# A routed expert layer behind attention on one core: the two largest experts in blocks of 384, 256 and a last one by count

## The chip, the cores and the metric

One core of a Trainium2 chip. The time is device microseconds (us) from the start of an execution to its end; lower is better. Engines are named as the profile names them: PE (TensorE, matrix products), DVE (VectorE), ACT (ScalarE), POOL (GpSimd) and SP (SyncE, which issues most transfers here).

## The reference, cut to what matters

```python
scores = np.matmul(z, z.transpose(0, 2, 1)) / S          # 8 batches, S = 1856, d_qk = 64
attn = np.maximum(scores, 0.0) ** 2
x = (u * np.matmul(attn, v)).reshape(8 * 1856, 256)       # 14848 tokens

g_logits = x @ w_group                                    # 4 groups, arg max, softmax weight g_w
e_logits = xg @ w_expert[g]                               # 4 experts in a group, arg max, weight e_w
h = np.maximum(xg[mask_e] @ w1[g, e], 0.0)                # 256 -> 1024
out[tok_idx] = (g_w * e_w)[:, None] * (h @ w2[g, e])      # 1024 -> 256
```

Every token goes to one of 16 experts. Routing the reference's inputs sends 1050 tokens to each of the two largest experts, 924 and 907 of them from the first seven batches, and from 1020 down to 749 to the others.

## The kernel before, in words

**Attention.** A batch is worked in four chunks of query columns (512, 512, 320, 512), a chunk in 15 key steps. In a step PE makes scores (`sc`), ACT and DVE square them and split them into a rounded part `ah` and a rest `al` (every product is made of float32 numbers split in two), and PE adds to the chunk's output `o`. `chunk_end` multiplies by `u` and sets the chunk's routing going. PE makes the logits (`pl`), ACT copies them to `lgp`, SP transposes them to `lgx`, DVE takes them up as `lgf` and works through some 15 small operations in `route`, PE counts places by three small products `pk`, DVE adds the experts' running ends `base` (`rk`, `df`, `di`), and POOL scatters the token rows, four indirect transfers a chunk, into a table `bucket` in device memory, in which each expert has a range of its own.

`defer(step, f)` and `gens` set at which key step each piece of this stands in the program; what falls behind the last step is put between the steps of the first expert blocks by `early`. The last chunk's logits stand 5 steps behind its end and its routing 8.

**Sorting ahead.** After the seventh batch `sort_experts` ranks the experts by their rows so far. For the two that lead, `base` is raised to at least 512 (`FRZ`), so that no token of the last batch can fall into their first 512 rows: these are settled, and can be read while the last batch is still routed.

**Experts.** `PARTS` cuts each expert, in that order of size, into blocks of rows. The last block of each of the first 15 experts has its width set at run time by the count: a `Switch` with 15 arms, one program text for each width in `WIDE` (512, 496, ... 288), the arms one behind the other. Blocks run in this order: the first of expert 0, the first of expert 1, then what is left of expert 0, of expert 1, and then expert after expert. A block is eight steps `f`. In a step PE makes six `ph` products (up, lines 775 to 777), ACT turns them into `hh` and DVE into the rest `hl`, and three steps later (`AHEAD`) PE makes six `y` products (down, lines 790 to 792). PE thus runs up to three steps ahead of ACT and DVE. At a block's end ACT copies `y` to `yp`, SP transposes to `yr`, DVE weights the rows (`yf`) and POOL scatters them to the output.

A block's input is loaded by `load_rows`: SP transposes rows of `bucket` into `xp` and loads `meta` (weight and token number). `join_block` makes of it, in three neighbouring steps of the block before, `meta` and `xf` (DVE), `xh_m` (ACT) and `xl_m` (DVE). The first step is f = 3, and f = 4 for the block in place `NEARLY` = 2. `more_rows` loads blocks ahead once no routing is left.

**The edge between the two halves.** In the second block, at f = 3, what is left of the routing is drained. Then DVE makes the counts (`counts`, `arms`, `overflow_count`), from which every engine reads the arm to take (`arm_i`) early in the third block. A region with arms holds its eight steps and the first three of the block behind it, and ends with a jump behind the last arm. PE alone is told of the arm beforehand (`hint`).

## Time and profile before

| | |
|---|---|
| median of 3 runs | 1501.58 us (1500.08 to 1502.61) |
| profiled execution | 1500.23 us, span of its instructions 1498.4 us |
| PE | busy 1479.4 us, 99% of the span, 7575 products |
| DVE, ACT, POOL | 74%, 67%, 20% of the span |
| attention | until about 829 us |
| experts 0 and 1 | about 817 to 928 us |
| granted PE clock | 1.00 of full from 0 to 1480 us |

Busy time of PE is an upper bound: ends of products are modelled, and consecutive products overlap. What a product costs is read from one start to the next. A bracket behind a row is the idle time ahead of it and what ended that.

### The profile page before, as it was taken

What the parts mean: (1) busy time and instruction counts of PE and PEld (TensorE: products, weight loads), DVE (VectorE), ACT (ScalarE), POOL (GpSimd) and SP (SyncE); (2) the same over time, 40 slices, a digit from 0 to 9 for tenths busy, and PEclk for the clock granted to TensorE, in tenths of its full rate; (3) what the DMA queues carried; (4) which work ended last, traced back from release to release, by engine and by line L of the source; (5) the groups of instructions that cost most, each with busy time, mean ns of one, the idle gap of its engine ahead of it and who ended that gap; (6) DMA issues with size and microseconds to landing.
All of it is one profiled execution on the core that took longest, in us unless ns stands there. A gap on an engine that the chain in (4) does not pass through costs nothing.

```text
span 1498.4 us, 23731 instructions
## 1 busy us (share of the span) xinstructions
PE 1479.4 (99%) x7575; PEld 1288.6 (86%) x7575; DVE 1109.1 (74%) x2659; ACT 1003.1 (67%) x1919; POOL 297.8 (20%) x346
## 2 busy tenths in 40 slices
PE   9999999999999999999999999999999999999997
PEld 7888888888888888888888789999888899889996
DVE  7888887888888988788898756666565666666663
ACT  7988888888888888888888435454444444444442
POOL 0011221121201111212103122222222222222222
PEclk9999999999999999999999999999999999999999
DMA  4423423333424334233584475776545765657541
GB/s 135 109 68 90 118 76 98 92 74 99 105 65 106 79 98 106 64 86 86 146 245 112 94 153 90 167 148 132 119 85 119 141 139 137 137 137 135 132 96 51
DMA packets 302314, 167.54 MB, mean 112 GB/s; under 512 B 238187, under 2 KB 281197, under 8 KB 301936
## 3 DMA queue, kind: packets, MB, share of 16 engines
q1 hardware_dynamic: 289616, 132.37, 40.5%
q0 software_dynamic: 11968, 30.91, 6.9%
q14 instruction: 283, 2.32, 0.6%
q8 instruction: 95, 1.56, 0.5%
q10 hardware_dynamic: 352, 0.39, 0.1%
HBM read 72.25 MB, written 41.60 MB: 76 GB/s over the span
## 4 chain that ended last, share of the span: by engine, by line
PE 88%; issue 3%; DVE 3%; ACT 2%; DMA 2%; SPq 1%; POOL 0%; DVEq 0%; POOLq 0%; ACTq 0%
PE o L388 13%; PE o L387 13%; PE o L390 12%; PE sc L348 6%; PE ph L777 6%; PE ph L775 6%; PE ph L776 6%; PE y L792 6%; PE y L790 6%; PE y L791 6%; PE sc L351 6%; DMA out_dram<-yf,meta 1%; PE pl L444 1%; PE pl L445 1%; DVE hl L780 0%
## 5 line engine op out<-in xcount | busy, mean ns | idle before, releaser
L779 ACT ACTIVATE hh<-ph 128x512 fp32r<-128x512 f32 (+11 forms) x296 | 149.4, 512 | 322.0 <-PE ph L777 241.1
L388 PE MATMUL o<-ah,vh 128*128 128x512 f32 (+1 forms) x960 | 354.5, 371 | 0.0
L387 PE MATMUL o<-ah,vl 128*128 128x512 f32 (+1 forms) x960 | 353.0, 370 | 0.9 <-DVE ah L364 0.7
L780 DVE SCALAR_TENSOR_TENSOR hl<-ph,hh 128x512 fp32r<-128x512 f32 (+11 forms) x296 | 169.2, 579 | 224.0 <-ACT hh L779 201.5
L367 DVE TENSOR_TENSOR al<-r,ah 128x512 fp32r<-128x512 f32 (+1 forms) x448 | 283.7, 634 | 14.8 <-ACT r L361 8.1
L352 ACT ACTIVATE r<-sc 128x512 f32<-128x512 f32 (+1 forms) x448 | 239.2, 553 | 79.9 <-PE sc L351 53.0
L390 PE MATMUL o<-al,vh 128*128 128x512 f32 (+1 forms) x896 | 274.5, 373 | 0.4 <-DVE al L367 0.3
L363 ACT ACTIVATE r<-r 128x512 f32<-128x512 f32 (+3 forms) x416 | 237.6, 590 | 4.2
L582 POOL DMA_INDIRECT bucket<-rows,di x120 | 128.3, 1069 | 546.4 <-DVE al L367 229.4
L795 POOL DMA_INDIRECT out_dram<-yf,meta x129 | 144.4, 1119 | 459.3 <-DVE yf L839 413.3
L777 PE MATMUL ph<-xl_m,w1h_e 128*128 128x512 f32 (+11 forms) x592 | 205.1, 346 | 1.7 <-DVE xl_m L756 1.7
L387 PEld LDWEIGHTS o<-ah,vl 128*128 128x128 f32 x960 | 180.3, 188 | 29.9 <-DVE ah L364 1.3
L775 PE MATMUL ph<-xh_m,w1l_e 128*128 128x512 f32 (+11 forms) x592 | 204.9, 346 | 1.0 <-issue 1.0
L388 PEld LDWEIGHTS o<-ah,vh 128*128 128x128 f32 x960 | 180.5, 188 | 28.4
L776 PE MATMUL ph<-xh_m,w1h_e 128*128 128x512 f32 (+11 forms) x592 | 204.6, 346 | 0.0
L792 PE MATMUL y<-hl,w_e 128*128 128x512 f32 (+11 forms) x576 | 199.8, 347 | 1.3 <-DVE hl L780 1.3
L790 PE MATMUL y<-hh,w_e 128*128 128x512 f32 (+11 forms) x576 | 199.4, 346 | 0.8 <-ACT yp L820 0.8
L791 PE MATMUL y<-hh,w_e 128*128 128x512 f32 (+11 forms) x576 | 199.3, 346 | 0.0
L364 DVE CAST ah<-r 128x512 fp32r<-128x512 f32 (+3 forms) x416 | 163.8, 399 | 41.9 <-ACT r L363 21.6
L390 PEld LDWEIGHTS o<-al,vh 128*128 128x128 f32 x896 | 162.8, 188 | 26.3 <-DVE al L367 1.3
L348 PE MATMUL sc<-zm,z2h 128*128 128x512 f32 (+1 forms) x480 | 178.5, 376 | 0.9 <-DVE r L356 0.4
L351 PE MATMUL sc<-zm,z2l 128*128 128x512 f32 (+1 forms) x448 | 166.5, 373 | 0.2 <-DVE z2l L902 0.2
(150 smaller groups left out, 2107.8 us busy)
## 6 DMA issues: line engine op xcount, KB each, us to landing
raw_e<-in_w_dram SPq DMA_DIRECT2D x64, 512.0 KB
ut<-in_uT_dram SPq DMA_DIRECT2D x24, 512.0 KB
vr<-in_v_dram SPq DMA_DIRECT2D x23, 512.0 KB
bucket<-padrow SPq DMA_DIRECT2D x16, 528.0 KB
zr<-in_zT_dram SPq DMA_DIRECT2D x47, 128.0 KB
ut<-in_uT_dram SPq DMA_DIRECT2D x8, 320.0 KB
vr<-in_v_dram SPq DMA_DIRECT2D x9, 256.0 KB
out_dram<-yf,meta POOLq DMA_INDIRECT x129
```

The source lines that it names most:

```text
L348: nc.tensor.matmul(ps[:, 0:w], z2h[:, ks], zm, start=True, stop=k == NKF)
L351: nc.tensor.matmul(ps[:, 0:w], z2l[:, ks], zm, start=False, stop=True)
L367: nc.vector.tensor_sub(out=al, in0=a, in1=f32(ah))
L387: nc.tensor.matmul(o, vl[:, dsl], ah, start=(at_ == 0), stop=False)
L388: newest[:] = [nc.tensor.matmul(o, vh[:, dsl], ah, start=False, stop=(at_ == NK - 1 and al is None))]
L390: nc.tensor.matmul(o, vh[:, dsl], al, start=False, stop=(at_ == NK - 1))
L775: nc.tensor.matmul(o, wt["l"][d][:, fs], xh[:, d, 0:W], start=(d == 0), stop=False)
L776: nc.tensor.matmul(o, wt["h"][d][:, fs], xh[:, d, 0:W], start=False, stop=False)
L777: nc.tensor.matmul(o, wt["h"][d][:, fs], xl[:, d, 0:W], start=False, stop=(d == ND - 1))
L790: nc.tensor.matmul(o, w2t[:, 1, dsl], hh[:, 0:W], start=(f == 0), stop=False)
L791: nc.tensor.matmul(o, w2t[:, 0, dsl], hh[:, 0:W], start=False, stop=False)
L792: nc.tensor.matmul(o, w2t[:, 0, dsl], hl_[:, 0:W], start=False, stop=(f == NF - 1))
```

## The change

`PARTS` gives experts 0 and 1 the blocks (384, 256, up to 512) of experts 2 to 4. With 1050 rows their last block has 410 rows and takes the arm of 416 (the seventh of 15); before, it had 282 and took 288, the fifteenth and last. The columns of the two experts stay the same: 512 + 256 + 288 = 384 + 256 + 416. `FRZ` settles 640 rows of expert 0 and 384 of expert 1, so three blocks can be loaded while routing goes on (`NFREE`). The last chunk's logits stand 7 steps behind its end instead of 5, its routing 10 instead of 8, and the drain and the counts at f = 6 of the second block. The later first step of a join, f = 4, falls to the fourth block, the last of expert 0.

```diff
-PARTS = ((512, 256, 512),) * 2 + ((384, 256, 512),) * 3 + ((512, 512),) * 8 + ((384, 512),) * 2 + ((512, 352),)
+PARTS = ((384, 256, 512),) * 5 + ((512, 512),) * 8 + ((384, 512),) * 2 + ((512, 352),)
...
-    FRZ = 512
-    assert all(p[0] == FRZ and len(p) > 1 for p in PARTS[:NEARLY])
+    NFREE = 3
+    FRZ = (640, 384)
+    assert sum(PARTS[0][:2]) == FRZ[0] and PARTS[1][0] == FRZ[1] and min(len(p) for p in PARTS[:NEARLY]) > 2
...
-        defer(s + (5 if last else 2), logits)
+        defer(s + (7 if last else 2), logits)
...
-        wait = 8 if last else 6
+        wait = 10 if last else 6
...
-        nc.vector.tensor_scalar(out=fz, in0=rank, scalar1=float(NEARLY), scalar2=float(FRZ),
+        nc.vector.tensor_scalar(out=fz, in0=rank, scalar1=1.0, scalar2=float(FRZ[0] - FRZ[1]),
                                 op0=ALU.is_lt, op1=ALU.mult)
         nc.vector.tensor_add(out=fz, in0=fz, in1=ebase)
+        fz1 = cst("sfz1", [P, NE])
+        nc.vector.tensor_scalar(out=fz1, in0=rank, scalar1=float(NEARLY), scalar2=float(FRZ[1]),
+                                op0=ALU.is_lt, op1=ALU.mult)
+        nc.vector.tensor_add(out=fz, in0=fz, in1=fz1)
         nc.vector.tensor_tensor(out=base, in0=base, in1=fz, op=ALU.max)
...
     def more_rows():
-        if not (deferred or gens):
-            while late["loaded"] < min(NB, late["joined"] + 2):
-                load_rows(late["loaded"])
-                late["loaded"] += 1
+        while late["loaded"] < min(NB if not (deferred or gens) else NFREE, late["joined"] + 2):
+            load_rows(late["loaded"])
+            late["loaded"] += 1
...
-            f0 = 4 if i + 1 == NEARLY else 3
+            f0 = 4 if i + 1 == NFREE else 3
...
-            if i + 1 == NEARLY and f == 3:
+            if i + 1 == NEARLY and f == 6:
...
-            if i + 1 < NB and f == (4 if i + 1 == NEARLY else 3) + 2:
+            if i + 1 < NB and f == (4 if i + 1 == NFREE else 3) + 2:
```

SP's queue behind the last chunk. `rows_3` and `lgx_3` are the last chunk's token rows and logits, `yr` the first block's output, `xp` and `meta` of 256 rows the input of the third block. Before:

```order
L434 DMA_TRANSPOSE rows_3_11160<-pl_3_11162 128x4x128 x4
L452 DMA_TRANSPOSE lgx_3_11164<-lgp_3_11163 128x8x48
L829 DMA_TRANSPOSE yr_0_11417<-yp_0_11414 128x4x128 x2
L829 DMA_TRANSPOSE yr_2_11423<-yp_2_11420 128x4x128 x2
L734 ISA
L734 DMA_TRANSPOSE xp_11445<-bucket 128x4x256
```

Now:

```order
L435 DMA_TRANSPOSE rows_3_11161<-pl_3_11163 128x4x128 x4
L453 DMA_TRANSPOSE lgx_3_11165<-lgp_3_11164 128x8x48
L739 ISA
L739 DMA_TRANSPOSE xp_11299<-bucket 128x4x256
L742 ISA
L742 DMA meta_11301<-bucket 128x2x2
L834 DMA_TRANSPOSE yr_0_11406<-yp_0_11403 128x4x128 x2
```

The third block's load moved ahead of the first block's output.

DVE in the second block. `hl_3` to `hl_7` are its steps; `meta`, `xf` and `xl_m` are the join of the third block; `cnt` is the first row of the counts, `ki` the last. Before:

```order
L1117 CAST ki<-tiles 128x1
L780 SCALAR_TENSOR_TENSOR hl_4_11485<-ph_4_11477,hh_4_11484 128x512
L763 TENSOR_TENSOR meta_11447<-meta_11447,none 128x2
L748 COPY xf_11495<-xp_11445 128x2x2x256
L780 SCALAR_TENSOR_TENSOR hl_5_11507<-ph_5_11499,hh_5_11506 128x512
L780 SCALAR_TENSOR_TENSOR hl_6_11525<-ph_6_11517,hh_6_11524 128x512
L756 TENSOR_TENSOR xl_m_11498<-xf_11495,xh_m_11497 128x2x256
```

Now:

```order
L785 SCALAR_TENSOR_TENSOR hl_3_11438<-ph_3_11430,hh_3_11437 128x384
L768 TENSOR_TENSOR meta_11301<-meta_11301,none 128x2
L753 COPY xf_11450<-xp_11299 128x2x2x256
L785 SCALAR_TENSOR_TENSOR hl_4_11462<-ph_4_11454,hh_4_11461 128x384
L785 SCALAR_TENSOR_TENSOR hl_5_11480<-ph_5_11472,hh_5_11479 128x384
L761 TENSOR_TENSOR xl_m_11453<-xf_11450,xh_m_11452 128x2x256
L785 SCALAR_TENSOR_TENSOR hl_6_11498<-ph_6_11490,hh_6_11497 128x384
L612 TENSOR_TENSOR cnt<-base,ebase 128x16
```

The counts moved behind the join and three steps back, the join a step ahead.

PE around the third chunk's places. `pk_2` are these, `ph_4` the first block's fifth step, `pl_3` the last chunk's logits. Before:

```order
L563 MATMUL pk_2_11112<-pre_2_11089,ones 128x16
L791 MATMUL y_0_11214<-hh_1_11187,w_e_0_9648 128x512
L792 MATMUL y_0_11214<-hl_1_11188,w_e_0_9648 128x512
L790 MATMUL y_1_11215<-hh_1_11187,w_e_0_9648 128x512
L791 MATMUL y_1_11215<-hh_1_11187,w_e_0_9648 128x512
L792 MATMUL y_1_11215<-hl_1_11188,w_e_0_9648 128x512
L444 MATMUL pl_3_11250<-xh_3_11152,whl 128x512
```

Now:

```order
L564 MATMUL pk_2_11113<-pre_2_11090,ones 128x16
L782 MATMUL ph_4_11233<-xl_m_10935,w1h_e_1_9644 128x384
L795 MATMUL y_0_11215<-hh_1_11188,w_e_0_9646 128x384
L796 MATMUL y_0_11215<-hh_1_11188,w_e_0_9646 128x384
L797 MATMUL y_0_11215<-hl_1_11189,w_e_0_9646 128x384
L795 MATMUL y_1_11216<-hh_1_11188,w_e_0_9646 128x384
```

Before, five products stood between the third chunk's last place count and `pl_3`; now the rest of that step and two whole steps do. The last chunk's own `pk_3` stands four steps behind `pl_3` now, and five before.

## Prediction

> **What bounds the kernel.** I read the page's busy times and its chain first.

> ```profile
> span 1498.4 us, 23731 instructions
> PE 1479.4 (99%) x7575; PEld 1288.6 (86%) x7575; DVE 1109.1 (74%) x2659; ACT 1003.1 (67%) x1919; POOL 297.8 (20%) x346
> PE 88%; issue 3%; DVE 3%; ACT 2%; DMA 2%; SPq 1%; POOL 0%; DVEq 0%; POOLq 0%; ACTq 0%
> ```

> PE sets the time: what the change gives or takes is products that cost more or less, and idle time of PE added or removed. The waits of PE, longest first, say how little idle time there is, and the timeline of PE where it is.

> ```profile
> PE ph L777 <- DVE xl_m L756: 1.7, 3, 1.2
> PE y L792 <- DVE hl L780: 1.3, 1, 1.3
> PE ph L775 <- issue: 1.0, 2, 0.6
> PE y L790 <- ACT yp L820: 0.8, 1, 0.8
> ```

> ```profile
> 765.70 0.50 PE L387 MATMUL o<-ah,vl 128*128 128x512 f32 x1 [0.31 <-DVE ah L364]
> ...
> 836.12 0.48 PE L444 MATMUL pl<-xh,whl 128*128 128x512 f32 x1 [0.68 <-DVE df L575]
> ...
> 848.56 0.18 PE L562 MATMUL pk<-pre,ones 128*128 128x48 bf16 x1 [0.33 <-DVE pre L544]
> ...
> 868.70 0.39 PE L777 MATMUL ph<-xl_m,w1h_e 128*128 128x256 f32 x1 [0.36 <-DVE xl_m L756]
> ...
> 871.23 0.37 PE L775 MATMUL ph<-xh_m,w1l_e 128*128 128x256 f32 x1 [0.40 <-issue]
> ...
> 888.15 0.29 PE L791 MATMUL y<-hh,w_e 128*128 128x288 f32 x1
> 889.71 0.40 PE L792 MATMUL y<-hl,w_e 128*128 128x288 f32 x1 [1.27 <-DVE hl L780]
> ...
> 902.33 0.37 PE L775 MATMUL ph<-xh_m,w1l_e 128*128 128x256 f32 x1 [0.58 <-issue]
> ...
> 924.02 0.44 PE L777 MATMUL ph<-xl_m,w1h_e 128*128 128x384 f32 x1 [1.16 <-DVE xl_m L756]
> ```

> So all the idle time that the two experts hold is seven short waits between 836 and 924 us. A wait costs more than its bracket: from 888.15 to 889.71 are 1.56 us where 0.13 are usual, 1.43 lost for a bracket of 1.27. I add 0.2 to each bracket: 0.9, 0.5, 0.6, 0.6, 1.5, 0.8 and 1.4, together 6.3 us. That is all the change can win here, 0.42%.

> **Products.** Each pair of rows below stands 24 products apart (512 and 384 wide) or 36 (288 and 416).

> ```profile
> 851.62 0.39 PE L775 MATMUL ph<-xh_m,w1l_e 128*128 128x512 f32 x1
> ...
> 857.06 0.39 PE L775 MATMUL ph<-xh_m,w1l_e 128*128 128x512 f32 x1
> ...
> 931.56 0.33 PE L775 MATMUL ph<-xh_m,w1l_e 128*128 128x384 f32 x1
> ...
> 935.72 0.33 PE L775 MATMUL ph<-xh_m,w1l_e 128*128 128x384 f32 x1
> ...
> 916.03 0.29 PE L775 MATMUL ph<-xh_m,w1l_e 128*128 128x288 f32 x1
> ...
> 920.77 0.29 PE L775 MATMUL ph<-xh_m,w1l_e 128*128 128x288 f32 x1
> ...
> 1213.80 0.35 PE L775 MATMUL ph<-xh_m,w1l_e 128*128 128x416 f32 x1
> ...
> 1220.52 0.35 PE L775 MATMUL ph<-xh_m,w1l_e 128*128 128x416 f32 x1
> ```

> That is 0.2267, 0.1733, 0.1317 and 0.1867 us a product; steps of twelve take 2.72, 2.08, 1.58 and 2.24. Before, 0.2267 + 0.1317 = 0.3583; now 0.1733 + 0.1867 = 0.3600. Times 96 products a block and two experts: **+0.3 us** (0 to +0.4, as the starts are rounded to 0.01). PE's work does not change; only the waits are left.

> ```profile
> 839.08 1.20 SPq L452 DMA_TRANSPOSE lgx<-lgp  x1
> 845.38 0.34 DVE L458 COPY lgf<-lgx 128x320 uint16<-128x320 uint16 x1
> 848.72 0.17 DVE L554 TENSOR_TENSOR rows<-ew,sm 128x4 f32<-128x4 f32 x1
> 857.24 0.17 DVE L611 TENSOR_TENSOR cnt<-base,ebase 128x16 f32<-128x16 f32 x1
> 860.06 0.17 DVE L633 CAST arm_i<-arm 128x15 int32<-128x15 f32 x1
> 865.34 0.16 DVE L763 TENSOR_TENSOR meta<-meta,none 128x2 int32<-128x2 int32 x1 [3.41 <-DMA meta<-bucket]
> 878.01 1.35 DVE L748 COPY xf<-xp 128x2048 uint16<-128x2048 uint16 x1
> 879.39 1.05 ACT L754 CAST xh_m<-xf 128x1024 fp32r<-128x1024 f32 x1 [1.08 <-DVE xf L748]
> 881.10 1.22 DVE L756 TENSOR_TENSOR xl_m<-xf,xh_m 128x1024 fp32r<-128x1024 f32 x1
> ```

> **The last logits (wait of 0.9 us).** `pl` needs the one bank that the third chunk's `pk` used, and DVE read it late. Two steps and a half, some 5 us, now stand between them in place of five products: **-0.9** (-0.9 to -0.5, if DVE lags).

> **The last places (0.5 us).** On DVE the chain from `lgf` to the row weights lasts 3.3 us (845.38 to 848.72) and starts behind a step's `hl`; `pk` stands behind two and a half more groups of six on PE. With six products at 1.04 instead of 1.36 that cover shrinks by three times 0.32, about 1.0; `hl` itself comes 0.2 sooner. **+0.8** (0 to +2; the upper end, if `lgx`, issued at 839.08 behind transposes that keep their place, is late for a routing that begins at about the same time as before: nine shorter steps for seven longer).

> **The third block's join (0.6 us).** DVE waited 3.41 us for a load that stood behind the drain and the first block's output on SP. It stands ahead of both now, four shorter steps before its use, and its rows wait for the third chunk's scatter alone: **-0.6** (-0.6 to 0).

> **Counts and arms (0.6 us at 871).** From `cnt` to `arm_i` are 3.0 us (857.24 to 860.06 and 0.17). They stand behind the seventh step of the second block in place of the fourth; PE reads the arm some one and a half steps later, about 4 us, so a little under 1 us is left of some 10. The read itself stays: **0** (0 to +1).

> **The fourth block's join.** Its first step is f = 4 instead of 3, in a block whose steps take 1.44 us. `xf`, `xh_m` and `xl_m` take 1.35 + 1.05 + 1.22 = 3.6 and one `hl` between; before, they ended at 882.32 for a region that starts about 882.7. From the step's own `hl`, some 1.5 us into it, they now end about 6.2 us into what are 6.1 to the first use: **+0.3** (0 to +1). Its load waits for the last scatter, but has four steps more than the one before.

> ```profile
> 889.20 0.46 DVE L780 SCALAR_TENSOR_TENSOR hl<-ph,hh 128x288 fp32r<-128x288 f32 x1 [6.17 <-ACT yp L820]
> ...
> 914.89 1.19 DVE L780 SCALAR_TENSOR_TENSOR hl<-ph,hh 128x288 fp32r<-128x288 f32 x3 [3.82 <-ACT hh L779]
> ...
> 1003.63 0.54 DVE L780 SCALAR_TENSOR_TENSOR hl<-ph,hh 128x368 fp32r<-128x368 f32 x1 [5.75 <-ACT hh L779]
> ```

> **Into the arm (1.5 us at 889).** These are DVE's first rows in the arms of experts 0, 1 and 3: it is away 3.8 to 6.2 us while PE lives on its three steps' lead. Three ups and three downs of the narrow block are 3 x (0.79 + 0.71) = 4.5 us of cover; at 416 wide 3 x (1.12 + 0.71) = 5.5, and one more up of 1.12 in place of 0.79: 1.3 us more. Against it, DVE leaves up to 1 us later, behind the later join. Expert 3's arm, away 5.75, put PE to no wait of 0.3 us, and the waits have only one of this kind. **-1.1** (-1.5 to 0).

> **Out of the arm.**

> ```profile
> 903.75 0.42 DVE L780 SCALAR_TENSOR_TENSOR hl<-ph,hh 128x256 fp32r<-128x256 f32 x1 [1.92 <-ACT hh L779]
> ...
> 978.29 0.56 DVE L780 SCALAR_TENSOR_TENSOR hl<-ph,hh 128x384 fp32r<-128x384 f32 x1 [3.39 <-ACT hh L779]
> ...
> 1069.25 0.69 DVE L780 SCALAR_TENSOR_TENSOR hl<-ph,hh 128x512 fp32r<-128x512 f32 x1 [4.43 <-ACT hh L779]
> ```

> Behind expert 0's arm, the last of the fifteen, DVE is back after 1.92 us; behind those of experts 2 and 4, with other arms' text between them and the exit, after 3.39 and 4.43. Experts 0 and 1 now leave from the seventh arm, so 1.5 to 2.5 us more. Behind expert 1 follow steps of 2.08, as behind expert 2, where PE did not wait. Behind expert 0 follow five of 1.44: about 4.3 us of lead against DVE's return, then `xf` of 1.35 and a weight split ahead of the next `xl_m`. **+0.6** (0 to +2.5); the 0.8 at 902.33 stays. [...]

> **Expert 2's first join (1.4 us at 924).** Its three steps now lie in a region with steps of 2.24 instead of 1.58, 2 us more: **-1.4** (-1.4 to -0.5).

> **Sorting.** Two more DVE operations while attention runs, where PE lost 0.5 at 765.70; each like this row:

> ```profile
> 761.41 0.17 DVE L671 TENSOR_SCALAR sfz<-srank 128x16 f32<-128x16 f32 x1
> ```

> **+0.2** (0 to +0.4). One output tile fewer for each of the two experts frees ACT, DVE and POOL off the path: 0.

> **The sum.** 0.3 - 0.9 + 0.8 - 0.6 + 0 + 0.3 - 1.1 + 0.6 - 1.4 + 0.2 = -1.8 us. The profiled execution took 1500.23 us; it would take 1498.4. The median stands 1.35 above it: 1501.58 - 1.8 = **1499.8 us**. A difference under 0.2%, 3 us, is about what cannot be told from none.

> **The rivals.** *The waits go and no new one comes*: places, fourth join and exit all covered, 1.7 us less: 1498.1, faster. For it speaks that behind 930 us PE's longest wait is the 0.8 for `yp`, at the same joins and arms; against it the narrow steps right behind an exit, which occur nowhere there.

> *The exits decide*: DVE and ACT come back from expert 0's new arm as late as they went in at 889 (6.17), the narrow block behind cannot cover it, about 2.5 to 3 lost, DVE's delay passes to expert 1's entry (1.5), and the 1.5 at 889 stay: -1.8 + 2.2 + 1.5 + 1.1 = +3.0, 1504.6, slower. It decides from an absence of about 6 us at this exit; the rows above reach 4.43. At the middle, 4.4 with the entry's wait kept, it gives about 1501.5, no change.

> *The change does not settle what it says*: with fewer than 640 rows sorted, gaps would be computed as rows. The routed counts, 924 and 907, exclude it.

> **Chances.** My sum, within 1.3 of it: 0.5. No new waits: 0.3. Exits, slower: 0.13; the rest lies between. The range reaches from 1496.8 (every gain, the issue waits gone too) to 1503.2 (exits at 4.4 to 5). Faster by over 0.2%: 0.35; within: 0.52; slower: 0.13.

> **What would show it.** The row of `pl` behind the last chunk without a bracket, that of `pk` with 1 us or more; no DMA wait of DVE ahead of the third block; PE's wait for `hl` in expert 0's arm under 0.5; DVE away 3 us or more behind that arm, and PE waiting for `hl` or `xl_m` there; none for `xl_m` ahead of expert 2. Wrong it is if the last routing arrives late and PE waits several us for `pk` or for the fourth block's rows.

## The result, and the profile after

The changed kernel takes 1511.85 us (median of seven executions, 1505.54 to 1513.71) against 1501.41 us of the kernel before on the same chip: ratio 1.0057, 95% interval 1.0044 to 1.007. It is slower, by more than the forecast's range allowed (1499.8, range 1496.8 to 1503.2). The profiled execution took 1511.61 us.

The page, and the longest waits of PE (in total, how often, the longest):

```profile
span 1509.9 us, 23735 instructions
PE 1486.7 (98%) x7575; PEld 1302.2 (86%) x7575; DVE 1106.9 (73%) x2661; ACT 1004.9 (67%) x1923; POOL 296.1 (20%) x340
PE 88%; issue 4%; DVE 3%; DMA 2%; ACT 2%; SPq 1%; POOL 0%; POOLq 0%; ACTq 0%; DVEq 0%
```

```profile
PE ph L780 <- issue: 3.3, 1, 3.3
PE ph L782 <- DVE xl_m L761: 2.7, 1, 2.7
PE ph L780 <- DVE hl L785: 1.7, 1, 1.7
...
PE y L797 <- DVE hl L785: 1.2, 1, 1.2
```

The timeline of PE at the places that the prediction spoke of:

```profile
838.26 0.39 PE L445 MATMUL pl<-xh,whl 128*128 128x512 f32 x1
...
848.56 0.20 PE L562 MATMUL pk<-oh,tri 128*128 128x64 bf16 x1 [0.48 <-DVE oh L527]
849.17 0.18 PE L563 MATMUL pk<-pre,ones 128*128 128x48 bf16 x1 [0.41 <-DVE pre L545]
...
863.46 0.37 PE L780 MATMUL ph<-xh_m,w1l_e 128*128 128x256 f32 x1 [1.66 <-DVE hl L785]
...
881.41 0.46 PE L795 MATMUL y<-hh,w_e 128*128 128x416 f32 x1 [0.24 <-ACT hh L784]
...
904.46 0.39 PE L797 MATMUL y<-hl,w_e 128*128 128x256 f32 x1
...
908.47 0.71 PE L780 MATMUL ph<-xh_m,w1l_e 128*128 128x416 f32 x1 [3.27 <-issue]
908.97 0.55 PE L781 MATMUL ph<-xh_m,w1h_e 128*128 128x416 f32 x1
909.32 0.55 PE L782 MATMUL ph<-xl_m,w1h_e 128*128 128x416 f32 x1
...
958.35 0.39 PE L797 MATMUL y<-hl,w_e 128*128 128x256 f32 x1 [1.18 <-DVE hl L785]
...
962.45 0.69 PE L782 MATMUL ph<-xl_m,w1h_e 128*128 128x384 f32 x1 [2.70 <-DVE xl_m L761]
962.93 0.52 PE L780 MATMUL ph<-xh_m,w1l_e 128*128 128x384 f32 x1
963.25 0.52 PE L781 MATMUL ph<-xh_m,w1h_e 128*128 128x384 f32 x1
```

The old waits are gone: `pl` stands without a bracket, the one inside expert 0's arm is 0.24 in place of 1.27, and none stands at 924. Two new ones are longer than any before: 3.27 us at the entry to expert 1's arm, 2.70 at the entry to expert 2's. Behind both the products lie farther apart: 416 wide 0.35 (908.97 to 909.32) in place of 0.187, 384 wide 0.48 and 0.32 in place of 0.173. The granted clock is lower in the same places. Windows of the trace (PEclk is the third number from the right), changed kernel first, then the kernel before at the same place:

```profile
905.00:914.00 9.00, 5.73 (x21) 5.36 (x20) 3.53 (x6) 0.90 (x2) 1.98 (x2) 0.62 0.78 155
962.00:969.00 7.00, 6.55 (x26) 6.55 (x27) 1.06 (x3) 0.98 (x2) 0.52 (x1) 0.54 1.34 201
```

```profile
905.00:914.00 9.00, 9.00 (x74) 8.85 (x74) 5.60 (x9) 2.26 (x5) 1.97 (x2) 1.00 0.80 122
```

The clock reads 0.50 over 907.2 to 913.8 and over 961.8 to 968.4, and 1.00 from 914.0 to 961.6 between them. Over the first window a mean of 0.62 is 6.8 us at half clock; the second stretch, from 961.66 on, is as long.

To see where the time went, I added up by stage what PE lost: each distance between the starts of two consecutive products, less the usual one of that width (14.5 ns and 0.415 ns a column, which gives the distances of the prediction, and 55 ns for `pk` and for the small products at the very start).

| PE lost, us | before | changed |
|---|---|---|
| 0 to 845 (attention, first block) | 16.4 | 16.9 |
| 845 to 858 (last places) | 0.7 | 1.4 |
| 858 to 870 (counts, third block) | 0.6 | 1.9 |
| 870 to 900 (expert 0's arm) | 2.3 | 0.9 |
| 900 to 922 (entry to expert 1's arm) | 0.9 | 6.4 |
| 922 to 945 | 1.5 | 0.0 |
| 945 to 975 (entry to expert 2's arm) | 0.3 | 7.6 |
| 975 to the end | 2.1 | 2.0 |
| sum | 24.9 | 36.9 |

The usual distances sum to 1462.65 us in both, as they must with a fixed price a column and the same columns, so the 12.0 us more are, to 0.5, the 11.5 by which the span grew. The two entries hold 12.8 of them. Of the 13.9 us lost at them now, the three waits are 7.6 (3.4, 1.3 and 2.9). Of the other 6.3 most is the half clock behind them: 5.4 and 6.0 us of the two stretches lie behind a wait, and half of that, 5.7, is my estimate, from the clock of 0.50, of the most that they cost. The one execution at 1505.54 us, 6.3 below the median, had a granted clock of 0.998 over the run, the other six 0.994 or 0.995.

### The profile page after: what moved, and what is told of

Read it like the earlier page. It is cut to its first block, busy times and chain, and to the rows that moved or that the text cites. A ratio compares the mean times of both kernels' runs of the same rounds, so it can differ in the third digit from the quotient of the medians.

```text
span 1509.9 us, 23735 instructions
## 1 busy us (share of the span) xinstructions
PE 1486.7 (98%) x7575; PEld 1302.2 (86%) x7575; DVE 1106.9 (73%) x2661; ACT 1004.9 (67%) x1923; POOL 296.1 (20%) x340
## 3 DMA queue, kind: packets, MB, share of 16 engines
q8 instruction: 95, 1.56, 0.5%
## 4 chain that ended last, share of the span: by engine, by line
PE 88%; issue 4%; DVE 3%; DMA 2%; ACT 2%; SPq 1%; POOL 0%; POOLq 0%; ACTq 0%; DVEq 0%
PE o L389 12%; PE o L388 12%; PE o L391 12%; PE ph L782 6%; PE ph L780 6%; PE ph L781 6%; PE y L797 6%; PE y L795 6%; PE y L796 6%; PE sc L349 6%; PE sc L352 6%; DMA out_dram<-yf,meta 1%; PE pl L446 1%; PE pl L445 1%; DVE al L368 1%
## 5 line engine op out<-in xcount | busy, mean ns | idle before, releaser
L784 ACT ACTIVATE hh<-ph 128x384 fp32r<-128x384 f32 (+10 forms) x296 | 149.7, 513 | 328.8 <-PE ph L782 252.4
L785 DVE SCALAR_TENSOR_TENSOR hl<-ph,hh 128x384 fp32r<-128x384 f32 (+10 forms) x296 | 169.2, 579 | 234.2 <-ACT hh L784 206.1
L364 ACT ACTIVATE r<-r 128x512 f32<-128x512 f32 (+3 forms) x416 | 238.3, 591 | 4.3
L800 POOL DMA_INDIRECT out_dram<-yf,meta x127 | 141.3, 1113 | 476.4 <-DVE yf L844 447.8
L780 PE MATMUL ph<-xh_m,w1l_e 128*128 128x384 f32 (+10 forms) x592 | 206.6, 349 | 5.0 <-issue 3.3
L782 PE MATMUL ph<-xl_m,w1h_e 128*128 128x384 f32 (+10 forms) x592 | 206.5, 349 | 2.8 <-DVE xl_m L761 2.7
L781 PE MATMUL ph<-xh_m,w1h_e 128*128 128x384 f32 (+10 forms) x592 | 205.9, 348 | 0.0
L797 PE MATMUL y<-hl,w_e 128*128 128x384 f32 (+10 forms) x576 | 200.8, 349 | 1.3 <-DVE hl L785 1.2
L795 PE MATMUL y<-hh,w_e 128*128 128x384 f32 (+10 forms) x576 | 200.4, 348 | 0.8 <-issue 0.5
L796 PE MATMUL y<-hh,w_e 128*128 128x384 f32 (+10 forms) x576 | 200.1, 347 | 0.0
```

The source lines that it names most:

```text
L780: nc.tensor.matmul(o, wt["l"][d][:, fs], xh[:, d, 0:W], start=(d == 0), stop=False)
L781: nc.tensor.matmul(o, wt["h"][d][:, fs], xh[:, d, 0:W], start=False, stop=False)
L782: nc.tensor.matmul(o, wt["h"][d][:, fs], xl[:, d, 0:W], start=False, stop=(d == ND - 1))
L795: nc.tensor.matmul(o, w2t[:, 1, dsl], hh[:, 0:W], start=(f == 0), stop=False)
L796: nc.tensor.matmul(o, w2t[:, 0, dsl], hh[:, 0:W], start=False, stop=False)
L797: nc.tensor.matmul(o, w2t[:, 0, dsl], hl_[:, 0:W], start=False, stop=(f == NF - 1))
```

## Where the new waits come from

In the changed kernel experts 0 and 1 leave their regions from the seventh of fifteen arms and not from the last. SP at the exit of expert 1's region, changed kernel: its last two output tiles, then the weights of expert 3; below that the instructions at the two ends of the jump (duration in ns, then start).

```profile
937.78 3.34 SPq L834 DMA_TRANSPOSE yr<-yp  x2
943.92 0.37 SPq L199 DMA_DIRECT2D raw_e<-in_w_dram  x1
```

```profile
L1350 SPq COMPARE_BRANCH  x1: 53/53/53, 941.2 to 941.2; - x1
```

```profile
L199 SPq FUSED_REGOPS  x1: 46/46/46, 943.7 to 943.7; - x1
```

From 941.17 to 943.69 SP does nothing, 2.52 us. The same in the kernel before:

```profile
933.05 1.21 SPq L829 DMA_TRANSPOSE yr<-yp  x1
935.07 0.36 SPq L198 DMA_DIRECT2D raw_e<-in_w_dram  x1
```

There the jump takes 0.45 us (934.39 to 934.84). The price was to be read in that trace all the same, one expert later: behind expert 2's arm, which isn't the last, SP's branch starts at 980.3 and its next instruction at 982.8.

```profile
L1346 SPq COMPARE_BRANCH  x1: 56/56/56, 980.3 to 980.3; - x1
```

```profile
L734 SPq FUSED_REGOPS  x1: 51/51/51, 982.8 to 982.8; - x1
```

SP is late for a second reason. The 416-wide block has four output tiles in place of three, and they stand on SP ahead of the exit. Together, SP issues expert 3's weights 11.2 us behind the end of PE's own exit branch (932.76 to 943.92), before 6.4 us (928.70 to 935.07). Behind the weights SP loads the rows of expert 2's last block:

```profile
945.72 6.93 SPq L739 DMA_TRANSPOSE xp<-bucket  x1
953.01 0.37 SPq L742 DMA_DIRECT2D meta<-bucket  x1
```

ACT waits for the weights, and DVE for the rows, whose join then goes on over ACT:

```profile
947.65 1.05 ACT L203 CAST w1h_e<-raw_e 128x1024 fp32r<-128x1024 f32 x1 [3.22 <-DMA raw_e<-in_w_dram]
...
951.40 1.15 ACT L215 CAST w_e<-raw_e 128x512 fp32r<-128x512 f32 x2 [2.14 <-DMA raw_e<-in_w_dram]
...
958.03 1.05 ACT L759 CAST xh_m<-xf 128x1024 fp32r<-128x1024 f32 x1 [3.13 <-DVE xf L753]
```

```profile
956.60 0.17 DVE L768 TENSOR_TENSOR meta<-meta,none 128x4 int32<-128x4 int32 x1 [1.18 <-DMA meta<-bucket]
961.18 1.21 DVE L761 TENSOR_TENSOR xl_m<-xf,xh_m 128x1024 fp32r<-128x1024 f32 x1
```

ACT's two waits for weights keep DVE behind until 955.4. The wait that ends last, though, is DVE's own for `meta`, 1.18 us; from there DVE, ACT and DVE work on to the `xl_m` for which PE waits. In the kernel before, the rows' load starts at 936.78 and takes 5.51 us, and DVE does not wait for it.

At expert 1's entry it is PE's own sequencer. Its branch into the arm, in the changed kernel and in the kernel before:

```profile
L1350 PEldq COMPARE_BRANCH  x1: 3571/3571/3571, 904.7 to 904.7; - x1
```

```profile
L1346 PEldq COMPARE_BRANCH  x1: 1767/1767/1767, 907.8 to 907.8; - x1
```

The hint for that arm is the first thing behind expert 0's exit (897.00 and 902.23). Counted from the hint, the branch is through after 11.3 us now and after 7.4 before. PE's sequencer gets to the branch 5.6 us behind the hint before and 7.7 now; before, PE's queued products covered the 1.8 us that were left, now they do not cover 3.6.

Experts 2 to 14 left from far arms before the change too, and PE loses only 2 us behind 975 us. What differs is the room. Into expert 2's arm PE's branch comes 25 us behind its hint and lasts 0.30 us (958.63), as whole blocks of that expert stand between; between expert 0's exit and expert 1's arm stand five narrow steps. And behind expert 2's exit, in the kernel before, no weights stand ahead of the rows on SP, whose load takes 2.03 us.

The theory for the runs: **an arm that isn't the last is a far exit, and the far exit makes SP and PE late at what follows.** The rivals: narrow first blocks and the moved routing and counts; or the longer last block by itself.

## Experiments

Times are medians. A ratio is the recorded one to the kernel before run beside it, with its interval; it is not the quotient of the two medians (for the changed kernel that would be 1.0070). The last four columns are PE's losses in one profiled execution, by the stages above.

| kernel | us | ratio (95%) | 858-870 | 900-922 | 945-975 | all |
|---|---|---|---|---|---|---|
| changed | 1511.85 | 1.0057 (1.0044 to 1.007) | 1.9 | 6.4 | 7.6 | 36.9 |
| near_exit | 1500.28 | 0.9985 (0.9975 to 0.9996) | 1.7 | 0.7 | 2.0 | 27.3 |
| settle_only | 1499.65 | 0.9988 (0.9978 to 0.9998) | 0.8 | 1.5 | 2.9 | 25.3 |
| only_second | 1504.12 | 1.0023 (1.001 to 1.0036) | 2.0 | 0.8 | 4.5 | 28.4 |
| before_far | 1503.04 | 1.0005 (0.9993 to 1.0016) | 0.5 | 6.1 | 5.9 | 34.3 |
| rotated | 1504.77 | 1.0021 (1.0008 to 1.0034) | 2.3 | 0.6 | 3.6 | 30.1 |
| late_cuts | 1509.83 | 1.0046 (1.0031 to 1.006) | 1.8 | 6.6 | 3.0 | 35.9 |
| before_no_hint | 1503.50 | 1.0014 (1.0003 to 1.0024) | 0.4 | 2.1 | 0.5 | 27.5 |
| after_no_hint | 1511.72 | 1.0065 (1.0051 to 1.008) | 1.8 | 6.4 | 7.3 | 36.4 |
| rotated_spread | 1502.61 | 1.0000 (0.9991 to 1.0008) | 1.0 | 0.7 | 5.5 | 28.9 |
| near_spread | 1498.24 | 0.9975 (0.9964 to 0.9987) | 0.1 | 0.7 | 0.3 | 21.4 |
| rotated_late | 1502.09 | 0.9999 (0.999 to 1.0008) | 3.8 | 0.2 | 1.3 | 26.0 |
| all_three | 1499.85 | 0.9992 (0.9979 to 1.0005) | 1.0 | 0.7 | 4.7 | 32.1 |

**near_exit**: the last arm again, by another cut.

```diff
-PARTS = ((384, 256, 512),) * 5 + ...
+PARTS = ((384, 384, 512),) * 2 + ((384, 256, 512),) * 3 + ...
-    FRZ = (640, 384)
+    FRZ = (768, 384)
```

> The changed kernel with the two largest experts in blocks of 384, 384 and a last one by count: the last block has 282 rows and takes the arm of 288 columns, the last of the fifteen in the program, as before the change; all the rest (settling ahead, moved counts) stays as changed, and so do the columns, 1056 for each. Far-exit theory (leaving a region from an arm in its middle makes PE and SP late at what follows): both stretches of half clock go, 908 us and 958 to 969 us, some 13 us of the 36.9 us that PE lost, and the 863 us wait may stay; time 1499 to 1503 us. Rival, narrow first blocks and counts made at the third block: the waits of about 3 us stay at both entries, 1508 to 1513 us. Second rival, late weights alone (the row writes of a longer last block hold SP): the wait at the third largest expert's entry goes, that at the second largest's stays, 1504 to 1507 us.

Neither entry has a wait of 3 us or half clock (a wait of 1.16 us is left at expert 2's), and the time is 0.15% under the kernel before, as the far-exit theory says. But this run changes the third block's width and the number of output tiles as well.

**settle_only**: the old widths with all the rest of the change.

```diff
-PARTS = ((384, 256, 512),) * 5 + ...
+PARTS = ((512, 256, 512),) * 2 + ((384, 256, 512),) * 3 + ...
-    FRZ = (640, 384)
+    FRZ = (768, 512)
```

> The changed kernel with the old blocks of the two largest experts (512, 256 and a last one of 288 by count) and 768 and 512 of their rows settled: the earlier routing and counts, the third block loaded early and the moved joins stay. Far-exit theory: 1498 to 1503 us, no wait of 3 us at an entry. Moved-work theory (the earlier settling and the counts at the third block cause the loss): 1507 to 1513 us.

The early settling and the moved routing are worth 0.12%; the rival that blames them for the whole loss falls.

**only_second**: expert 0 as before, expert 1 at 416.

```diff
-PARTS = ((384, 256, 512),) * 5 + ...
+PARTS = ((512, 256, 512),) + ((384, 256, 512),) * 4 + ...
-    FRZ = (640, 384)
+    FRZ = (768, 384)
```

> The changed kernel with the largest expert back at 512, 256 and 288 by count (last arm) and only the second largest at 384, 256 and 416 (arm 6). Far-exit theory: the entry to the second largest's last block (behind a near exit) is free, the entry to the third largest's blocks (behind the far exit) keeps its waits of 1.2 and 2.7 us and its half clock, about +7 us: 1505 to 1509 us. Late-fetch theory by the entered arm (the wait belongs to entering arm 6, not to leaving it): the wait of 3.3 us at the second largest's entry stays as well, 1509 to 1513 us. Moved-work theory: 1508 to 1513 us with waits elsewhere.

Expert 1's entry is clear (0.8) though PE enters the seventh arm; what costs is the exit that came before. The entry to expert 2, behind the far exit, keeps a wait of 2.69 us. The time is a little under the expected range.

**before_far**: the kernel before, with its arms written from narrow to wide.

```diff
-WIDE = tuple(range(512, 287, -16))
+WIDE = tuple(range(288, 513, 16))
...
-in1=left.unsqueeze(2).to_broadcast([P, NDYN, NW - 1]), op=ALU.is_ge,
+in1=left.unsqueeze(2).to_broadcast([P, NDYN, NW - 1]), op=ALU.is_lt,
```

> The kernel before, with the fifteen arms written from 288 up to 512 columns in place of 512 down to 288: the two largest experts still run 288 columns, but in the first arm, with fourteen arms between its end and the code that follows; nothing else differs in work, blocks or timing. Far-exit theory: waits of about 3 us appear at the entry of the second largest's last block (about 909 us) and the third largest's first or last block (about 953 us), each followed by half clock, 1507 to 1514 us. Rivals (narrow blocks, moved counts, a longer last block): 1500 to 1503 us, as before.

The profiled execution (1510.06 us) shows both new waits, with nothing changed but the order of the arms. First its PE from 880 to 975 us, then its branch into expert 1's arm:

```profile
PE ph L775 <- issue: 3.3, 1, 3.3
PE ph L777 <- DVE xl_m L756: 2.7, 1, 2.7
```

```profile
L1346 PEldq COMPARE_BRANCH  x1: 3591/3591/3591, 907.0 to 907.0; - x1
```

The median missed: 1503.04, a ratio that cannot be told from 1, and the twelve executions run from 1499.46 to 1510.06, with a granted clock over the run from 0.999 down to 0.994. So a far exit alone is able to make both waits, and does not make them, or the half clock, every time. Why the changed kernel shows the full loss in six executions of seven and this one in one or two of twelve is not settled.

**rotated**: all of the change, and the arm of 416 written last.

```diff
-WIDE = tuple(range(512, 287, -16))
+WIDE = tuple(range(432, 513, 16)) + tuple(range(288, 417, 16))
...
+        wrap = sq("wrap")[:, 0, 0:NDYN]
+        nc.vector.tensor_scalar(out=wrap, in0=arm, scalar1=8.5, scalar2=-15.0, op0=ALU.is_gt, op1=ALU.mult)
+        nc.vector.scalar_tensor_tensor(out=arm, in0=arm, scalar=6.0, in1=wrap, op0=ALU.add, op1=ALU.add)
```

> The changed kernel with all of the change in it, 384, 256 and 416 columns too, but its fifteen arms written in another order: 432 to 512, then 288 to 416, so that the arm which the two largest experts take is the last in the program. Two small DVE operations more make the arm's number. Far-exit theory: SP goes on 0.45 us behind its branch out of that arm in place of 2.52, PE's branch into the second largest's arm lasts 1 to 2 us in place of 3.57, both stretches of half clock go, and the time is 1499 to 1502 us, some 11 us under the changed kernel. Rivals (the longer last block with its four output tiles, the blocks' widths, the moved counts): the wait at the third largest's entry stays, 1505 to 1512 us.

SP's branch out of expert 1's arm, and PE's into it:

```profile
L1353 SPq COMPARE_BRANCH  x1: 53/53/53, 937.4 to 937.4; - x1
```

```profile
L1353 PEldq COMPARE_BRANCH  x1: 1782/1782/1782, 905.0 to 905.0; - x1
```

SP goes on 0.45 us later (937.39 to 937.85). The arm's place is thus the larger part: from 1.0057 to 1.0021, 0.36% or 5.4 us, with the blocks the same. That is about what expert 1's entry had lost more; it loses 0.6 now. The forecast of 1499 to 1502 missed, though: 3 us are left, with a wait of 1.86 us at expert 2's entry and 2.2 us lost at 865. With the jump short, SP still issues expert 3's weights 9.4 us behind PE's exit (928.63 to 938.07), 3 us later than in the kernel before; the fourth tile is what stands there more.

**late_cuts**: more time for the weights that SP issues late.

```diff
-    CUTS = {2: (0, 7, 9, 12), 3: (0, 4, 6, 9), ...}
+    CUTS = {2: (0, 7, 9, 12), 3: (0, 6, 8, 11), ...}
```

> The changed kernel with the weights of the fourth largest expert split 0, 6, 8 and 11 steps behind the second largest's region in place of 0, 4, 6 and 9: their transfers, which SP issues behind its exit from that region, get two steps (4.2 us) more before ACT and DVE wait for them. If SP's late exit (2.52 us, behind four output tiles) is what makes PE wait 2.7 us for xl_m at the third largest's last block, that wait and the half clock behind it go: 1504 to 1508 us, with the 3.3 us at the second largest's entry left. If it is DVE's or ACT's own way out of the arm, nothing changes: 1509 to 1513 us.

Expert 2's entry loses 3.0 us in place of 7.6, without the half clock, but not nothing: a wait of 2.3 us for `hl` took the place. The time fell by 2 us only and stays above what was expected. The late weights are a part of that wait. What is left is the rows behind them: ACT no longer waits for weights, but DVE waits 4.12 us for `meta` (957.07).

**before_no_hint** and **after_no_hint**: no hint of expert 1's arm.

```diff
-                hint(e + 1, (PE,))
+                if e:
+                    hint(e + 1, (PE,))
```

> The kernel before without the hint to PE of the second largest expert's arm (the one for every other expert stays). [...] Theory that the hint was too late or lost in the changed kernel: PE's branch lasts 3 to 4.5 us here too, in place of 1.77, PE waits 2.5 us or more at the entry, and if the clock halves it is 1504 to 1508 us. Rival, the hint does nothing: unchanged, 1500 to 1503 us, branch of 1.8 us.

> The changed kernel without the hint to PE of the second largest expert's arm. If the hint behind a far exit is lost, the branch at the entry stays at 3.6 us and the time at 1509 to 1513 us. If the hint's transfer is only late (it ended 11.3 us behind the hint, against 7.4 in the kernel before), the branch without it lasts longer, and so do the wait and the stretch of half clock: branch 4.5 us or more, 1511 to 1516 us.

The branch, without the hint, in the kernel before and in the changed one:

```profile
L1347 PEldq COMPARE_BRANCH  x1: 3960/3960/3960, 907.6 to 907.6; - x1
```

```profile
L1351 PEldq COMPARE_BRANCH  x1: 4562/4562/4562, 904.4 to 904.4; - x1
```

So the hint is worth 2.2 us of branch in the kernel before (3.96 against 1.77) and 1.0 in the changed one (4.56 against 3.57): behind the far exit it isn't lost, its branch is through later. What the expectation of after_no_hint takes for the end of a transfer, 11.3 and 7.4 us behind the hint, is the end of that branch. Over the profiled executions with the hint, the branch is through 7.4 to 9.0 us behind the hint where expert 0's exit is near (before 7.4, settle_only 7.4, only_second 7.9, rotated 8.0, near_exit 9.0), and 11.0 to 11.3 where it is far (before_far 11.0, late_cuts 11.2, changed 11.3). PE waited 2.09 us in before_no_hint, a little under what was expected, and the clock stayed at 1.00; its 1503.50 us lie between the two expected ranges. In after_no_hint the wait grew to 4.42 us as expected, but the stretch of half clock behind it is shorter than with the hint (3.4 against 6.8 us), and the time is the same.

**rotated_spread**: the counts' work cut in three.

```diff
                 counts()
-                arms()
-                overflow_count()
+            if i + 1 == NEARLY and f == 7:
+                arms()
...
+            if i == NEARLY and f == 1:
+                overflow_count()
                 load_arms()
                 hint(0, (PE,))
```

> The kernel called rotated (all of the change, the taken arm last) with the counts' work on DVE cut in three: counts behind the seventh step of the second block, the arms behind the eighth, the overflow's count and the reading of the arms behind the second step of the third block. In rotated PE lost 2.2 us at 865 us, where the reading of the arms (1.8 us on PE's sequencer) began only when DVE had the arms, about 861 us. If the moved counts are what cost there, that wait falls to 0.5 us or less and the kernel gains 1.5 to 2 us: 1502 to 1503.5 us. Rival, another wait takes its place (hl behind the arms, the hint of the first arm too late): 1504 to 1506 us.

In the changed kernel PE's reading of the arm starts the moment DVE has made it, and takes 1.79 us of its sequencer. The bracket of the row at 863.46 names `hl`, but that was done by 862.9; PE's sequencer was at the reading until 862.75 and at the hint behind it until 863.41.

```profile
860.75 0.17 DVE L634 CAST arm_i<-arm 128x15 int32<-128x15 f32 x1
```

```profile
L1202 PEldq TENSOR_LOAD <-arm_i x1: 1786/1786/1786, 861.0 to 861.0; - x1
```

With the work spread, the time fell by 2.2 us, as expected; the loss there fell from 2.3 to 1.0, less far than expected. At expert 2's entry this execution waits 2.69 us with a near exit: SP's load of the rows took 6.86 us, against 5.53 in rotated, and DVE waited 2.04 us for `meta`. **near_spread** is near_exit with the same edit.

> The kernel called near_exit (384, 384 and 288 columns) with the same cut of the counts. Same theory: the loss of 1.6 us at 863 us goes and the time is 1498 to 1499.5 us, faster than before the change by 0.15 to 0.25%. Rival: 1500 to 1501 us.

There the loss at 863 is gone (1.7 to 0.1). At 1498.24 us, ratio 0.9975, this kernel beats both: the change's settling, the last arm kept, the counts spread.

**rotated_late**: rotated with late_cuts' edit.

> The kernel called rotated with the fourth largest expert's weights split 0, 6, 8 and 11 steps behind the second largest's region, as in late_cuts. Theory: what is left of the cost at the third largest's entry (1.9 us of wait and a stretch at a lower clock, 3.6 us lost between 945 and 975 us) comes of SP, which passes four output tiles of the wide last block before it issues those weights; with two steps more the loss there falls under 1.5 us and the time to 1501 to 1503.5 us. Rival, the join behind the longer last block is late by itself: 1504 to 1506 us.

The stage of expert 2's entry loses 1.3 in place of 3.6, and the time falls to that of the kernel before. With the near exit it does what it did only by half in late_cuts: there SP stood 2.61 us at the exit, here 0.45, and DVE waits 1.23 us for `meta` in place of 4.12.

**all_three**: rotated with both edits.

> All of the change (384, 256 and 416 columns, settling, moved routing) with the three costs found so far taken out together: the taken arm written last, the counts cut in three, the fourth largest expert's weights split two steps later. If far exits, counts and SP's late weights are all that the change lost, PE loses some 23 to 25 us in all, like the kernel before (24.9) or a little less, and the time is 1499 to 1501.5 us, near the 1499.8 forecast. If something else of the wide last block still costs, 1502 to 1504 us.

The median is 1499.85 us, inside the first range. The profiled execution was one of two at about 1507; nine of the eleven lie at 1502.2 or below. It had waits of 1.88 and 2.34 us at the entries to experts 0's and 2's arms, each with half clock behind it, so its 32.1 us lost do not speak for the median. At the second, SP's load of the rows took 7.50 us (5.27 in rotated_late), and DVE waited 4.17 for `meta`: moving the weights does not help when the rows come late. Why that load takes from 5 to 7.5 us is open.

## Why the prediction was wrong

The signs that the prediction named came about nearly as it said (the two brackets of `pk` come to 0.9 us), and the time still left its range: none of them looked at SP, or at PE's branch.

**The step that failed is "Out of the arm".** It asked what a far exit costs DVE, and got the size right: DVE was away 3.82 us behind expert 0's arm and PE lost 0.3 us for it (0.6 were forecast).

```profile
901.20 0.42 DVE L785 SCALAR_TENSOR_TENSOR hl<-ph,hh 128x256 fp32r<-128x256 f32 x1 [3.82 <-ACT hh L784]
```

```profile
900.78 0.39 ACT L784 ACTIVATE hh<-ph 128x256 fp32r<-128x256 f32 x1 [1.74 <-PE ph L782]
```

Even there the wait that ended last was ACT's: DVE begins as ACT's `hh` ends (901.17), and ACT had been idle for 1.74 us though its `ph` was done at 898.34.

But it never asked the same of the other queues that take the jump. SP's row stood in the trace of before (2.5 us behind expert 2's arm, 0.45 behind expert 0's); PE's had to be seen in the length of its branch into expert 1's arm, 1.77 us just covered, which left nothing for a branch that is through 4 us later behind its hint (11.3 us against 7.4). In place of +0.6 stand +5.5 at expert 1's entry and a part of the +7.3 at expert 2's, where 3.3 are left in rotated and 5.2 in rotated_spread though the exit is near. SP pays at the exit itself, 2.5 us against 0.45. PE's own exit branch is no longer than before (1.97 against 2.34 us at expert 0's); PE pays at the next arm, 7.4 to 9.0 against 11.0 to 11.3 us behind the hint.

**"One output tile fewer ... off the path: 0"** failed too. On SP the number of tiles stays (121 transposes of `yr` in both traces; only POOL's scatters to the output fell, from 129 to 127): one tile moved from the first block into the last, and there it stands ahead of the exit and the weights. The 0 named no work that hides it. rotated_late takes 3.3 us off by ratio (1.0021 to 0.9999) once those weights have time, though its profiled execution also found the rows sooner on SP (5.27 us), so not all of it need be the weights'.

**Counts and arms: 0 (bound +1).** It was +1.2, and 3.2 us by the ratios of rotated and rotated_spread. The step counted DVE's 3 us against PE's distance but left out that PE's own reading of 1.79 us starts only then.

**Nothing had a price for the clock.** Over 5 of the 12 us are, by the estimate of 5.7 above, half clock behind the waits; a sum of waits alone would have come out at little more than half the loss even with the right waits.

The other steps held. `pl` runs without a wait; `pk` costs 0.7 more (0.8 forecast); the join of the third block has no wait; expert 0's arm and its surroundings lose 1.5 us less (1.1 forecast, with 0.6 of the moved counts); the 1.5 us at 924 are gone. The +0.3 of the products cannot be tested with a fixed price a column. The fourth block's join costs nothing (0.3 forecast).

**The rivals.** "The exits decide" had the right cause and the right sign with a chance of 0.13, but named DVE at expert 0's exit and a turning point of 6 us away. DVE's absence stayed at 3.8, and it was decided by SP and PE. With the three costs out, the median is 1499.85, beside the 1499.8 forecast (ratio 0.9992 where the forecast's is 0.9988); two of the edits take out losses that the kernel before also had in part (0.6 at the counts), so this agrees with the other terms rather than proves each.

## What to carry to other kernels

Where a change moves which arm of a switch runs, or where in the program code stands, price the jump on every engine that takes it, the queue that issues transfers (2.52 us here in place of 0.45) and PE's next hinted branch (3.57 in place of 1.77) included, and ask what each issues next and how soon the next arm or load is needed: behind experts 2 to 14, where there is room, the same kind of jump left PE with 2.0 us lost in all. A place with no wait is not a place with room: look for how long the covered branch or load lasts before putting more behind it. And a new wait of PE is to be priced with the half clock that may follow: in these fourteen traces it followed all nine losses from 2.8 us on (waits of 2.69 us or more), and five of nine of 2.0 to 2.5 us.

## What the runs showed of the hardware

```profile
880.00:890.00 10.00, 8.12 (x35) 7.30 (x34) 5.95 (x12) 4.38 (x9) 3.07 (x3) 0.83 0.67 131
```

```profile
959.00:969.00 10.00, 9.49 (x53) 9.20 (x54) 7.68 (x15) 5.28 (x11) 3.37 (x3) 1.00 0.45 116
```

Waits of 2.69 us or more brought it each time. Of the shorter ones, 1.86 us (rotated) and 1.88 (all_three) did; 2.09 (before_no_hint) and 2.10 (settle_only) did not.

**A hinted arm took longer behind a far exit.** Where PE was hinted directly behind a far exit, its branch was through 11.0 to 11.3 us behind the hint, behind a near one 7.4 to 9.0. Between the hint and that end the traces of the two kernels have two packets of 16 KB on the instruction queue q8, from 897.5 and 905.6 in the changed kernel, from 902.7 and 906.7 in the one before: the second starts 8.6 us behind the hint now and 4.5 before. Whose text they carry the traces do not say.
